# LSH attention with a routed expert layer: the second expert's number and first weight loads move ahead of the first expert's late rows

## The chip, the cores and the metric

The kernel runs on one core of a Trainium2 chip. The metric is the device time of one execution in microseconds (us). Before the change it is 733.53 us, the median of 3 runs (731.56 to 736.64). The profiled execution is a further one and took 737.76 us.

## The reference

Two stages follow one another. The first is attention over 4 batches, 8 heads, 768 positions and 64 values per head, in which a query sees only the keys of its own hash bucket (the signs of 6 projections). The second sends each of the 3072 tokens to one of 8 experts.

```python
# attention, per head
mask = q_bucket[:, :, :, None] == k_bucket[:, :, None, :]
scores = np.where(mask, scale * q @ k.T, -1e9)
x = softmax(scores) @ v                      # 3072 tokens x 512

# experts: one per token, by the largest logit
logits = x @ w_gate                          # 512 x 8
expert = argmax(logits, axis=1)
gate = softmax(logits)[token, expert]
for e in range(8):                           # w1: 512 x 1024, w2: 1024 x 512
    y[rows of e] = relu(x[rows of e] @ w1[e]) @ w2[e]
out = gate * y
```

All arrays are float32.

## The kernel before, in words

Attention works through 16 pairs of heads. Its work is issued by hand-written lists of steps (`HEAD`, `NEXT`, `PLAN`, `LAST`). Tokens are routed while attention still runs: each token's 512 values, its gate weight and its number are scattered into a DRAM table `sorted_rows` that has a region per expert (`scatter`, L501, indirect DMAs issued by POOL).

The experts are then handled one after the other, the fullest first, in phases (`PH`). Phase 0 takes the first 256 rows of the first expert, and overlaps the end of attention. Phase 1 takes its other 256 rows, the late rows. Phases 2 to 8 take one further expert each, 456 rows and fewer. Which expert comes when is known only on the chip: `rank_all` sorts the experts by their counts on DVE and writes the order to a tile `oi`, and `nc.values_load` (L562) has SP read a number out of `oi` into a register, so that later DMAs on SP can address that expert's weights.

A phase has two products. `mm1` (L774) makes eight blocks of hidden values, f = 0 to 7, each in one of three PSUM buffers named `s`. For each f, `relu` then takes the block out of PSUM twice: ACT writes the rounded value (`hh`, L788), and DVE the rest that rounding lost (L790). `mm2` multiplies by w2. In phases 0 and 1 it does so by tokens (`yout`, L831): 24 matmuls per 128 tokens, the last three of which read block f = 7. The three `s` buffers go round, so that the first `yout` of phase 1 writes the buffer that block f = 5 had.

Weights come in chunks of 128x4x512 float32: for the expert of rank r, chunks 4r and 4r+1 hold w1, chunks 4r+2 and 4r+3 hold w2. A chunk arrives in two loads of 128x2x512 (512 KB) each, which SP issues (`raw_load(c, a)`, L666) into small buffers `raw` and `raw2`. Each load has two parts, and `chunk_part(c, a)` splits a part into two tiles that TensorE multiplies: ACT rounds it (L679), POOL subtracts (L680). `halves(n, k)` splits part k of the two chunks from n on, and after each second part issues the load that takes the freed buffer. The loads of the second expert's w1 are (4, 0), (4, 1), (5, 0) and (5, 1). Parts 4 and 5 of its eight come with load (5, 0), parts 6 and 7 with load (5, 1).

`rows(n)` loads the tokens of phase n from `sorted_rows`: for phase 1 two DMAs of 128x578 float32 (L704, tile `xd`), for a later phase four of 32x16x128 (L698, tile `xg`, 256 KB each, in runs of 512 bytes) and one of 128x4x2 (L700, `xi`, in runs of 8 bytes). `xt` then transposes the late rows on TensorE (L736) in the middle of phase 0's second `yout`.

SP issues all these DMAs in program order through one queue, and an instruction that waits holds back all that stand behind it. When attention is done, its buffers are given up and a second pool (`p2`) takes their place. Tiles `raw2`, `xg`, `xi` and the later phases' tiles are in `p2`. Load (5, 0) goes to `raw2`, whose place is that of `xd`: it waits until the late rows have landed and TensorE has read them.

Of the kernel before, what the change touches and what calls it, by code (L numbers as in the profile page):

```python
# [23 lines left out]
E = 8  # L24
# [23 lines left out]
def tiles_of(n):  # L48

    return [(o, min(128, n - o)) for o in range(0, n, 128)]  # L50
# [3 lines left out]
def lsh_attention_moe(ctx, tc, qk2, v, proj, wg, w1, w1q, w2, out):  # L54
    nc = tc.nc
# [80 lines left out]
    C = {}  # L136
# [376 lines left out]
    SP = [mybir.EngineType.SP]  # L513
    EV = {}

    def keys(name):
        k = const.tile([128, E], F32, name=name)
        nc.vector.tensor_tensor(k, C["base"], C["base0"], op=OP.subtract)
        C["cnt"] = const.tile([128, E], F32, name=name + "_c")
        nc.vector.tensor_copy(C["cnt"], k)  # L520
        nc.vector.scalar_tensor_tensor(k, k, float(E), C["desc"], op0=OP.mult, op1=OP.add)
        return k
# [18 lines left out]
    def rank_all():  # L541
        k = keys("key1")
        nc.vector.scalar_tensor_tensor(k, C["first"], float(1 << 20), k, op0=OP.mult, op1=OP.add)
        g = const.tile([128, E, E], F32, name="rg")
        nc.vector.tensor_tensor(g, k[:, None, :].to_broadcast([128, E, E]), k[:, :, None].to_broadcast([128, E, E]),
                                op=OP.is_gt)
        rk = const.tile([128, E], F32, name="rk")
        nc.vector.tensor_reduce(rk, g, axis=AX.X, op=OP.add)
        ri = C["desc"]

        nc.vector.tensor_scalar(rk, rk, -1.0, float(E), op0=OP.mult, op1=OP.add)
        nc.vector.tensor_tensor(g, rk[:, None, :].to_broadcast([128, E, E]), ri[:, :, None].to_broadcast([128, E, E]),
                                op=OP.is_equal)
        C["rank_eq"] = g
        h = const.tile([128, E, E], F32, name="rh")
        nc.vector.tensor_tensor(h, g, C["desc"][:, None, :].to_broadcast([128, E, E]), op=OP.mult)
        od = const.tile([128, E], F32, name="od")
        nc.vector.tensor_reduce(od, h, axis=AX.X, op=OP.add)
        oi = const.tile([128, E], I32, name="oi")
        nc.vector.tensor_scalar(oi, od, -1.0, float(E), op0=OP.mult, op1=OP.add)  # L560
        for r in range(1, E):
            EV[r] = nc.values_load(oi[0:1, r:r + 1], engines=SP, min_val=0, max_val=E - 1)  # L562

    def spill_plan():

# [85 lines left out]
    def raw_load(c, a):  # L651

        r, k = divmod(c, 4)
        if k < 2:
            w = w1q if r else w1
            src = w[bass.ds(EV[r], 1)].rearrange("o (a p) f -> p (o a) f", p=128)[:, 2 * a:2 * a + 2,
                                                                               k * 512:(k + 1) * 512]
        else:
            o = (k - 2) * 4 + 2 * a
            src = w2[bass.ds(EV[r], 1)].rearrange("o (a p) d -> p (o a) d", p=128)[:, o:o + 2, :]  # L660
        n = 2 * c + a
        if n < 10 or n % 2:
            t = moe.tile([128, 2, 512], F32, name="raw", bufs=2)
        else:
            t = P2["p"].tile([128, 2, 512], F32, name="raw2", bufs=2)
        nc.sync.dma_start(t, src)  # L666
        RAW[c, a] = t

    def chunk_part(c, a):

        if a == 0:
            s = c % 6
            CH[c] = (moe if s < 4 else P2["p"]).tile([128, 2, 4, 512], F32R, name=CN[s])
        w, r = CH[c], RAW[c, a // 2][:, a % 2]
        if c < 4:
            nc.gpsimd.tensor_copy(w[:, 0, a], r)
            nc.gpsimd.tensor_tensor(w[:, 1, a], r, w[:, 0, a], op=OP.subtract)
        else:
            nc.scalar.activation(w[:, 0, a], r, AF.Copy)  # L679
            nc.gpsimd.tensor_tensor(w[:, 1, a], r, w[:, 0, a], op=OP.subtract)  # L680
# [8 lines left out]
    def rows(n):  # L689

        r, o, c = PH[n]
        if n > 1:
            XG[n] = P2["p"].tile([128, 16, 2 * D], F32, name="xg", bufs=2)
            XI[n] = P2["p"].tile([128, 4, 2], F32, name="xi", bufs=2)
            t = len(tiles_of(c))
            x = xsv[bass.ds(EV[r], 1), 0:128 * t]
            for a in range(4):
                nc.sync.dma_start(XG[n][32 * a:32 * a + 32, :4 * t][:, None],  # L698
                                  x[:, :, a * PW + E:a * PW + E + 2 * D].rearrange("o (g i) w -> i o g w", i=32))
            nc.sync.dma_start(XI[n][:, :t][:, None], x[:, :, GC:RW].rearrange("o (j p) w -> p o j w", p=128))  # L700
            return
        XG[n] = wk.tile([128, 2, RW], F32, name="xd")
        for j, (i, _) in enumerate(tiles_of(c)):
            nc.sync.dma_start(XG[n][:, j], xsv[bass.ds(EV[r], 1), o + i:o + i + 128].rearrange("o p w -> p (o w)"))  # L704

    def tokens(n):
        r, o, c = PH[n]
        IX[n] = moe.tile([128, 4], I32, name="ix", bufs=3)
        t = len(tiles_of(c))
        x = XI[n][:, :t, 1] if n > 1 else XG[n][:, :t, GC + 1]  # L710
        nc.vector.tensor_copy(IX[n][:, :t], x.bitcast(I32))
# [5 lines left out]
    def blocks(n, j):  # L717

        if j == 0:
            XT[n] = P2["p"].tile([128, 4, 512], F32, name="xt")  # L720
        if j < len(tiles_of(PH[n][2])):
            nc.vector.transpose(XT[n][:, :, 128 * j:128 * j + 128].rearrange("p c (t i) -> p t c i", i=32),
                                XG[n][:, 4 * j:4 * j + 4].rearrange("p t w -> p (t w)"))

    def xt(n, d):
        r, o, c = PH[n]
        if d == 0:
            XH[n] = (moe.tile([128, 2, 4, EARLY], F32R, name="xhe") if n < 2 else
                     P2["p"].tile([128, 2, 4, CAPS[1]], F32R, name="xh"))
        t = len(tiles_of(c))  # L730
        if n > 1:
            p = XT[n][:, d]
        else:
            p = ps.tile([128, 512], F32, name="t", bufs=2)
            for j in range(t):
                nc.tensor.transpose(p[:, j * 128:(j + 1) * 128], heads(XG[n][:, j], d), ident)  # L736
        if d == 0:
            GT[n] = moe.tile([128, 4], F32, name="gate", bufs=3)
            nc.vector.tensor_copy(GT[n][:, :t], XI[n][:, :t, 0] if n > 1 else XG[n][:, :t, GC])
            tokens(n)  # L740
        nc.scalar.activation(XH[n][:, 0, d, :c], p[:, :c], AF.Copy)
        nc.vector.tensor_tensor(XH[n][:, 1, d, :c], p[:, :c], XH[n][:, 0, d, :c], op=OP.subtract)  # L742
# [49 lines left out]
    def by_token(n):  # L792
        return PH[n][2] <= 384
# [288 lines left out]
    for g in range(NG):  # L1082
        for w in {0: HEAD, 1: NEXT, NG - 1: LAST}.get(g, PLAN):
# [6 lines left out]
            if g == NG - 1 and w == "R9":  # L1090
                GT[0] = moe.tile([128, 4], F32, name="gate", bufs=3)
                nc.vector.tensor_copy(GT[0][:, :2], XG[0][:, :, GC])
                tokens(0)
    rows(1)
    rank_all()
    raw_load(4, 0)
    raw_load(4, 1)
    def xts(n, ds):
        for d in ds:
            xt(n, d)  # L1100

    mm2(0, 0)
    mm2(0, 1, lambda: xts(1, (0, 1)))
    xts(1, (2, 3))
    attn.close()
    p2 = ExitStack()
# [5 lines left out]
    def halves(n, k):  # L1112

        if n < 4 * E:
            chunk_part(n + k // 4, k % 4)
            if k % 2:
                h = 2 * n + k // 2 + 3
                if h < LASTH:
                    raw_load(h // 2, h % 2)
# [6 lines left out]
    for n in range(1, len(PH)):  # L1126
        c0 = 4 * (PH[n][0] + 1)
        last = n + 1 == len(PH)
        if not last:
            rows(n + 1)  # L1130
        for f in range(8):
            mm1(n, f)
            if f % 2 and not by_token(n - 1):
                yout(n - 1, f // 2)
            halves(c0, f)
            if 3 <= n < 6:
                for _ in range(2):
                    next(plan, None)
        for m in range(4):
            mid, end = ((), ()) if last else (WHEN if n > 1 else SOON)[m]  # L1140
            if m == 0 and not last:
                for j in range(4):
                    blocks(n + 1, j)
            if not (last and m == 3):
                mm2(n, m, lambda: xts(n + 1, mid))
            halves(c0 + 2, 2 * m)
            halves(c0 + 2, 2 * m + 1)
            xts(n + 1, end)
        if n == 6:
            for _ in plan:  # L1150
                pass
        if n == 7:
            C["n"] = nc.values_load(C["cntn"][0:1, 0:1], min_val=0, max_val=TMAX)
# [65 lines left out]
```

## Time and profile before

| what | us |
|---|---|
| median of 3 runs | 733.53 |
| profiled execution | 737.76 |
| its span, first to last instruction | 735.9 |
| TensorE (PE) busy in the span | 706.5 |
| DVE busy | 490.0 |
| POOL busy | 486.3 |
| ACT busy | 413.7 |
| mean granted TensorE clock | 0.988 |

The span is what the profile's clock runs over: a moment of 461.90 is 461.90 us after the first instruction. The profiled execution takes 1.9 us more than its span, and 4.2 us more than the median of the runs. PE is the matmul side of TensorE, PEld its weight loads. SPq is SP's instruction stream; its rows are times of issue, not of transfer.

### The profile page before, as it was taken

Reading aid. Unit: us, or ns where it says so; the run is one execution under the profiler, and the core shown is the slowest. Engines: PE = TensorE matmul, PEld = TensorE weight load, DVE = VectorE, ACT = ScalarE, POOL = GpSimd, SP = SyncE. Lnnn points to the kernel's source line nnn. Section 1 sums busy time; section 2 is a strip of 40 time slices with the busy share of each in tenths; the row PEclk is TensorE's granted clock in tenths of the full one; section 3 lists DMA queues with packets and bytes.
Section 4 is the critical chain, followed back from the end, with each engine's and each line's share of the span. In section 5 each row is a group of like instructions: output and inputs, shape, how many; then the busy total and the mean of one; then the engine's idle time right before and its main releaser. Section 6 shows DMA issues by size and latency. Waiting matters only on the chain.

```text
span 735.9 us, 13469 instructions
## 1 busy us (share of the span) xinstructions
PE 706.5 (96%) x4575; PEld 571.2 (78%) x4575; DVE 490.0 (67%) x942; ACT 413.7 (56%) x836; POOL 486.3 (66%) x723
## 2 busy tenths in 40 slices
PE   8998999999999999999998999999999999999996
PEld 4766677667766776686666778799999999989895
DVE  7768898889888988998998663323666725232321
ACT  5876676677667866786676623443444444444310
POOL 8726766687778677876785664585666676768522
PEclk7999999999999999999999999999999999999998
DMA  5883788869777767797678337682737395747201
GB/s 196 289 287 78 240 242 233 250 193 257 193 214 214 221 168 224 217 257 178 193 204 219 108 133 205 193 244 88 199 132 176 135 140 180 194 145 209 75 10 39
DMA packets 69927, 135.58 MB, mean 184 GB/s; under 512 B 15571, under 2 KB 32211, under 8 KB 69856
## 3 DMA queue, kind: packets, MB, share of 16 engines
q1 hardware_dynamic: 63024, 118.31, 57.5%
q0 software_dynamic: 6688, 16.35, 6.5%
q8 instruction: 37, 0.61, 0.4%
q14 instruction: 34, 0.28, 0.1%
q10 hardware_dynamic: 144, 0.03, 0.0%
HBM read 75.79 MB, written 26.33 MB: 139 GB/s over the span
## 4 chain that ended last, share of the span: by engine, by line
PE 74%; DVE 8%; ACT 7%; issue 6%; DMA 2%; POOL 2%; SPq 1%; ACTq 0%; POOLq 0%; another core or an unknown queue 0%; DVEq 0%
PE t L407 17%; PE s L774 17%; PE s L811 10%; PE s L831 7%; PE t L346 7%; PE s L306 7%; PE s L308 6%; DVE m L316 4%; ACT e L332 4%; PE t L426 2%; DMA raw<-in_w1q_dram 1%; SPq L396 1%; ACT pt L372 1%; PE s L840 1%; ACT bits L241 1%
## 5 line engine op out<-in xcount | busy, mean ns | idle before, releaser
L332 ACT ACTIVATE e<-s,m 128x768 f32<-128x768 f32 x192 | 189.8, 992 | 80.6 <-DVE m L323 43.6
L316 DVE TENSOR_REDUCE m<-s 128x1 f32<-128x768 f32 x192 | 178.4, 947 | 14.8 <-PE s L308 9.4
L680 POOL TENSOR_TENSOR w<-raw,w 128x512 fp32r<-128x512 f32 x112 | 145.1, 1321 | 41.8 <-ACT w L679 41.0
L407 PE MATMUL t<-pt,vt 128*64 128x384 f32 x768 | 130.9, 490 | 0.2 <-DMA pt<-w 0.2
L774 PE MATMUL s<-xh,w 128*128 128x456 f32 (+6 forms) x672 | 127.0, 346 | 0.2 <-DVE xh L742 0.2
L774 PEld LDWEIGHTS s<-xh,w 128*128 128x128 f32 x672 | 119.1, 188 | 3.5 <-DVE xh L742 0.5
L790 DVE SCALAR_TENSOR_TENSOR hh<-s,hh 128x256 fp32r<-128x256 f32 (+7 forms) x64 | 35.5, 555 | 105.5 <-ACT hh L788 98.0
L346 PE MATMUL t<-ident,e 128*128 128x128 f32 x648 | 94.1, 276 | 8.3 <-ACT pt L372 2.7
L407 PEld LDWEIGHTS t<-pt,vt 128*64 128x64 f32 x768 | 52.4, 137 | 64.0 <-issue 62.7
L346 PEld LDWEIGHTS t<-ident,e 128*128 128x128 f32 x648 | 75.4, 141 | 20.7 <-ACT pt L372 6.3
L788 ACT ACTIVATE hh<-s 128x256 fp32r<-128x256 f32 (+7 forms) x64 | 31.3, 490 | 93.6 <-PE s L774 92.0
L386 DVE STREAM_TRANSPOSE w<-e 128x768 f32<-128x768 f32 x84 | 78.5, 959 | 8.2 <-ACT e L332 8.1
L811 PE MATMUL s<-hh,w 128*128 128x456 f32 (+3 forms) x384 | 74.9, 355 | 0.0
L811 PEld LDWEIGHTS s<-hh,w 128*128 128x128 f32 x384 | 71.1, 188 | 2.6
L321 POOL TENSOR_SCALAR m<-m 128x1 f32<-128x1 f32 x95 | 22.0, 232 | 75.8 <-DVE m L316 65.9
L679 ACT ACTIVATE w<-raw 128x512 fp32r<-128x512 f32 x112 | 66.4, 622 | 8.7 <-DMA raw<-in_w1q_dram 8.2
L372 ACT ACTIVATE pt<-t 128x512 f32<-128x512 f32 (+1 forms) x119 | 67.0, 586 | 6.3 <-PE t L346 5.5
L844 POOL DMA_INDIRECT out_dram<-y,ix x26 | 27.0, 1038 | 59.3 <-DVE y L842 26.0
L306 PE MATMUL s<-qk 80*128 80x384 f32 x192 | 57.1, 380 | 5.1 <-ACT e L332 4.8
L306 PE MATMUL s<-w 80*128 80x384 f32 x192 | 56.2, 374 | 5.0 <-ACT e L332 5.0
L831 PE MATMUL s<-w,hh 128*128 128x512 f32 (+1 forms) x240 | 56.7, 395 | 1.5 <-ACT hh L788 1.5
L831 PEld LDWEIGHTS s<-w,hh 128*128 128x128 f32 (+1 forms) x240 | 44.5, 187 | 12.4 <-ACT hh L788 1.9
(219 smaller groups left out, 1070.2 us busy)
## 6 DMA issues: line engine op xcount, KB each, us to landing
pt<-w SPq DMA_DIRECT2D x224, 144.0 KB
raw<-in_w_dram SPq DMA_DIRECT2D x36, 512.0 KB
raw<-in_w1q_dram SPq DMA_DIRECT2D x28, 512.0 KB
w<-in_qk_dram SPq DMA_DIRECT2D x14, 768.0 KB
xd<-in_qk_dram SPq DMA_DIRECT2D x14, 768.0 KB
sorted_rows<-xr SPq DMA_DIRECT2D x8, 1156.0 KB
vt<-in_v_dram SPq DMA_DIRECT2D x16, 384.0 KB
xg<-sorted_rows SPq DMA_DIRECT2D x16, 256.0 KB
```

The source lines that it names most:

```text
L306: nc.tensor.matmul(p[:, a, :HALF], k[0:80, 2, c], k[0:80, 3, n], start=i >= 4, stop=i < 4)
L316: nc.vector.tensor_reduce(m[:, 0:1], p[:, :, :HALF], axis=AX.XY, op=OP.max, negate=True)
L332: nc.scalar.activation(e, p[:, :, :HALF], AF.Exp, bias=m[:, 2:3], scale=m[:, 1:2], accum_out=SM[g, hf][:, t, s:s + 1])
L346: nc.tensor.transpose(p[:, x * 128:(x + 1) * 128], e[w][:, kt // 3, (kt % 3) * 128:(kt % 3) * 128 + 128], ident)
L372: nc.scalar.activation(o, x, AF.Copy)
L386: nc.vector.transpose(d.rearrange("p b k q -> p k b q"), PP.pop(i).rearrange("p a c -> p (a c)"))
L407: nc.tensor.matmul(p[s * 64:(s + 1) * 64, :HALF], VT[g][:, kt, s, :], x, start=(kt == 0), stop=(kt == NT - 1))
L679: nc.scalar.activation(w[:, 0, a], r, AF.Copy)
L680: nc.gpsimd.tensor_tensor(w[:, 1, a], r, w[:, 0, a], op=OP.subtract)
L774: nc.tensor.matmul(p[:, :c], w[:, a, d, fs], x[:, b, d, :c], start=(k == 0), stop=(k == 11))
L811: nc.tensor.matmul(p[:, :c], w[:, a, f % 4, ms], h[b][:, f, :c], start=(k == 0), stop=(k == 23))
L831: nc.tensor.matmul(p[:pw], HH[n][b][:, f, i:i + pw], w[:, a, f % 4], start=(k == 0), stop=(k == 23))
```

## The change

`rank_all` no longer loads the seven numbers. A new function `expert(r)` loads one. After attention, `rank_all` and `expert(1)` now run first, then the loads (4, 0) and (4, 1), and only then `rows(1)`. The numbers of ranks 2 to 7 are loaded in phase 1, behind `rows(2)`. In phase 1 alone, `halves` runs two parts ahead: parts 0 and 1 are split before `mm1`'s first block, part f + 2 behind block f, and nothing behind blocks 6 and 7.

```diff
-        for r in range(1, E):
-            EV[r] = nc.values_load(oi[0:1, r:r + 1], engines=SP, min_val=0, max_val=E - 1)
+        C["oi"] = oi
+
+    def expert(r):
+
+        EV[r] = nc.values_load(C["oi"][0:1, r:r + 1], engines=SP, min_val=0, max_val=E - 1)
...
-    rows(1)
     rank_all()
+    expert(1)
     raw_load(4, 0)
     raw_load(4, 1)
+    rows(1)
...
         if not last:
             rows(n + 1)
+        ahead = 2 if n == 1 else 0
+        if n == 1:
+            for r in range(2, E):
+                expert(r)
+        for k in range(ahead):
+            halves(c0, k)
         for f in range(8):
             mm1(n, f)
             if f % 2 and not by_token(n - 1):
                 yout(n - 1, f // 2)
-            halves(c0, f)
+            if f + ahead < 8:
+                halves(c0, f + ahead)
```

Only SP's and ACT's streams change; the order of instructions on PE, DVE and POOL is the same. SP's stream before, from the end of attention (`xd` is the late rows, `oi` the order of the experts, `raw`, `raw`, `raw_5697` and the last `raw` are loads (4, 0), (4, 1), (5, 0) and (5, 1); six more pairs of number loads and three more `xg` are left out):

```order
L704 DMA xd<-sorted_rows 128x578
L704 ISA
L704 DMA xd<-sorted_rows 128x578
L562 TENSOR_LOAD oi
L562 ISA x2
...
L666 DMA raw<-in_w1q_dram 128x2x512
L666 ISA
L666 DMA raw<-in_w1q_dram 128x2x512
L666 ISA
L666 DMA raw_5697<-in_w1q_dram 128x2x512
...
L700 DMA xi<-sorted_rows 128x4x2
L666 ISA
L666 DMA raw<-in_w1q_dram 128x2x512
```

SP's stream in the changed kernel (lines are 3 higher; (5, 0) is `raw_5637`; the first number load is that of rank 1, five of the six later pairs are left out):

```order
L565 TENSOR_LOAD oi
L565 ISA x2
L669 ISA
L669 DMA raw<-in_w1q_dram 128x2x512
...
L707 DMA xd<-sorted_rows 128x578
...
L669 DMA raw_5637<-in_w1q_dram 128x2x512
...
L703 DMA xi<-sorted_rows 128x4x2
L565 TENSOR_LOAD oi
L565 ISA x2
...
L669 DMA raw<-in_w1q_dram 128x2x512
```

Two weight loads now stand ahead of the late rows, and six number loads between `xi` and load (5, 1), the last of the four.

ACT's stream in phase 1 before, from the fifth block on (`hh` is a block's rounded value; `w<-raw_5697` is the split of load (5, 0), the last `w<-raw` that of load (5, 1)):

```order
L788 ACTIVATE hh_5706<-s 128x256
L679 ACTIVATE w_5796<-raw_5697 128x512
L788 ACTIVATE hh_5706<-s 128x256
L679 ACTIVATE w_5796<-raw_5697 128x512
L788 ACTIVATE hh_5706<-s 128x256
L679 ACTIVATE w_5796<-raw 128x512
L788 ACTIVATE hh_5706<-s 128x256
```

ACT's stream in the changed kernel, the same blocks (here from the third block):

```order
L791 ACTIVATE hh_5713<-s 128x256
L682 ACTIVATE w_5766<-raw_5637 128x512
L791 ACTIVATE hh_5713<-s 128x256
L682 ACTIVATE w_5766<-raw_5637 128x512
L791 ACTIVATE hh_5713<-s 128x256
L682 ACTIVATE w_5766<-raw 128x512
L791 ACTIVATE hh_5713<-s 128x256
L682 ACTIVATE w_5766<-raw 128x512
L791 ACTIVATE hh_5713<-s 128x256 x2
```

The first split of load (5, 1) stood between the blocks 6 and 7. It now stands between the blocks 4 and 5.

## Rows read from the trace of the kernel before

**Rows 1.** The page: busy us, share of the span and instructions of each engine.
```profile
PE 706.5 (96%) x4575; PEld 571.2 (78%) x4575; DVE 490.0 (67%) x942; ACT 413.7 (56%) x836; POOL 486.3 (66%) x723
```

**Rows 2.** Windows by stage: length, busy time (instructions) of each engine, clock, DMA.
```profile
440.00:476.50 36.50, 34.90 (x200) 29.73 (x198) 13.19 (x33) 14.89 (x32) 17.54 (x19) 1.00 0.69 199
476.50:720.00 243.50, 243.45 (x1291) 229.24 (x1292) 107.04 (x181) 96.95 (x192) 157.27 (x152) 1.00 0.54 147
```

**Rows 3.** Timeline of PE, 437 to 477: start, length, group, and idle time before it.
```profile
448.38 0.60 PE L736 MATMUL t<-ident,xd 128*128 128x128 f32 x4
...
450.28 11.78 PE L774 MATMUL s<-xhe,w 128*128 128x256 f32 x96
461.90 5.03 PE L831 MATMUL s<-w,hh 128*128 128x512 f32 x21
468.42 6.53 PE L831 MATMUL s<-w,hh 128*128 128x512 f32 x27 [1.50 <-ACT hh L788]
...
476.55 0.68 PE L774 MATMUL s<-xh,w 128*128 128x456 f32 x2 [0.15 <-DVE xh L742]
```

**Rows 4.** Chain of waits, 410 to 530: start, length, what the end waited for.
```profile
458.24 9.21 DMA raw<-in_w1q_dram
...
467.47 0.63 ACT w L679
468.10 0.28 ACT hh L788
```

**Rows 5.** Timeline of SP's queue, 395 to 486: start and length of issue.
```profile
443.42 0.90 SPq L704 DMA_DIRECT2D xd<-sorted_rows  x2
449.22 1.87 SPq L666 DMA_DIRECT2D raw<-in_w1q_dram  x3
451.31 4.36 SPq L698 DMA_DIRECT2D xg<-sorted_rows  x4
455.85 2.13 SPq L700 DMA_DIRECT2D xi<-sorted_rows  x1
458.24 2.36 SPq L666 DMA_DIRECT2D raw<-in_w1q_dram  x1
...
483.02 1.93 SPq L698 DMA_DIRECT2D xg<-sorted_rows  x4
485.14 0.82 SPq L700 DMA_DIRECT2D xi<-sorted_rows  x1
```

**Rows 6.** Waits of SP's queue, 405 to 500: total, times, longest.
```profile
SPq L704 <- DMA sorted_rows<-xr,slot: 18.1, 2, 16.7
```

**Rows 7.** The line of the number loads: duration (min/median/max in ns), first and last start.
```profile
L562 SPq TENSOR_LOAD <-oi x7: 261/269/481, 444.4 to 448.4; - x7
```

**Rows 8.** Timeline of DVE, 405 to 490.
```profile
440.87 0.17 DVE L560 TENSOR_SCALAR oi<-od 128x8 int32<-128x8 f32 x1
...
447.18 0.17 DVE L739 COPY gate<-xd 128x2 f32<-128x2 f32 x1 [2.51 <-DMA xd<-sorted_rows]
...
468.40 0.42 DVE L790 SCALAR_TENSOR_TENSOR hh<-s,hh 128x256 fp32r<-128x256 f32 x1 [6.91 <-ACT hh L788]
```

**Rows 9.** Windows by transfer: the last three columns are clock, DMA share, GB/s.
```profile
443.00:444.40 1.40, 1.40 (x7) 1.13 (x6) 0.48 (x1) 0.00 (x0) 0.00 (x0) 1.00 0.06 8
444.40:446.60 2.20, 2.20 (x11) 1.77 (x10) 0.27 (x1) 0.00 (x0) 1.06 (x2) 1.00 0.86 281
450.40:453.00 2.60, 2.60 (x24) 2.60 (x23) 1.43 (x4) 1.32 (x4) 0.98 (x1) 1.00 0.94 343
...
458.00:463.00 5.00, 5.00 (x39) 4.83 (x39) 1.27 (x3) 1.97 (x5) 3.19 (x3) 1.00 1.18 174
464.00:468.00 4.00, 2.92 (x13) 2.05 (x11) 0.00 (x0) 0.53 (x1) 0.00 (x0) 1.00 1.03 366
```

**Rows 10.** Windows around an earlier idle stretch of PE.
```profile
67.40:69.10 1.70, 0.04 (x7) 0.00 (x0) 1.63 (x5) 1.10 (x3) 0.88 (x2) 1.00 1.00 217
...
69.60:73.00 3.40, 3.40 (x15) 3.39 (x15) 2.21 (x6) 3.38 (x7) 2.06 (x4) 0.50 1.02 210
```

## The prediction, made before the changed kernel ran

> **What bounds the kernel now.** I read the busy table first: the matmuls fill 96% of the span, the next engine 67% [rows 1]. So only what shortens or moves TensorE's idle time can count. The table by stage then shows where that idle time is around the change: in 440 to 476.5 the matmuls are busy for 34.90 of 36.50 us, and in the 243.5 us after it for 243.45 [rows 2]. What the change could free is therefore the 1.6 us of its own stage; later stages have nothing to give, and a delay made here is not won back there.
>
> TensorE's timeline names the 1.6 us: 1.50 us before 468.42, where `yout` of the late rows waits for an ACT result, and 0.15 us before 476.55 [rows 3]. The chain of waits shows what is behind the 1.50: load (5, 1) is issued at 458.24 and lands 9.21 us later; ACT splits it (467.47) and only then takes out the last hidden block [rows 4]. SP's timeline shows why the load is late: SP does nothing from 444.32 to 449.22 but read seven numbers, and then four weight loads and all rows of the second expert go out in a heap [rows 5, 7].
>
> **SP's stream.** `oi` is written at 441.04 [rows 8]. SP is idle there: until 443.42 it waits for the scatters, the longest of the two waits being 16.7 us [rows 6]. Seven numbers take from 444.4 to 448.4 for six steps, 0.67 us each, and 0.8 us pass from the last one to the first load [rows 5, 7]. In the changed kernel one number is read at 441.1, load (4, 0) goes out at 441.9 (before: 449.22), (4, 1) at about 442.6, and the late rows at 443.42 as before. For SP this costs nothing: the wait for the scatters covers it. If the scatters landed 0.5 us earlier, the rows would be held back by the difference.
>
> **The late rows.** They now stand behind 1 MB of weights in the queue. Before, they are issued at 443.42, move from 444.4 to 446.6 at 281 GB/s [rows 5, 9], and DVE sees them at 447.18 [rows 8]; TensorE uses them at 448.38 [rows 3], 1.2 us later. In the changed kernel the weights start 1.0 us after their issue, at 442.9, and 1.05 MB at 343 to 366 GB/s [rows 9] take 2.9 to 3.1 us, until about 445.9. The 0.59 MB of rows follow at 281 GB/s: 2.1 us, and 0.6 us until they are seen, 448.6. A 256 KB output write goes on beside them and may take 0.7 us of that. TensorE then waits for 0.2 to 0.9 us. Bounds: nothing (the rows pass the weights), and 1.2 us (a slower start). I take **0.6 us**. It moves everything behind it, so below all times are relative to TensorE's.
>
> **Load (5, 0)** lies where the late rows lie, and waits for the transposes in both kernels: 450.7 (the third issue of 449.22 + 1.87 [rows 5]). It is not earlier, and `xg` and `xi` behind it are not either.
>
> **Load (5, 1)**, the one that TensorE waits for, is not issued earlier. Its buffer would be free two parts sooner, but six number loads now stand ahead of it on SP: `xg` from 451.3 for 1.93 us and `xi` 0.82 us (as in the next phase, where the queue is emptier [rows 5]), then 6 x 0.67 us, 458.3. Before: 458.24. What is gained is a shorter queue. By the rates of rows 9: the load (5, 0) moves from 451.8 on, 0.52 MB in 1.5 us; `xg`, 1.05 MB in short runs, at 174 GB/s in 6.0 us; (5, 1) in 1.4 us; 0.6 us to be seen: **461.3**. The same sum for the kernel before (1.57 MB from 450.4 in 4.5 us, then 6.0, 1.4, 0.6) gives 462.9, and it landed at 467.45 [rows 4], 4.55 us later than the sum. No row explains this lag; it could be that some DMA engines fall behind. So the lag is bounded by 0 and 4.55. It arose with 3.1 MB in the queue, and 2.1 MB are left: 4.55 x 2.1 / 3.1 = 3.1, hence landing at **464.4**; bounds 461.3 and 465.9.
>
> What a page says of such a load speaks for an earlier landing. The Trainium skill, "DMA: Bandwidth & Descriptors", section "Anatomy of one DMA", fits a DMA of its software path by about 2.0 us and the bytes at 436 GB/s, an estimated 3.2 us for 512 KB; landing would be at 461.5. This trace does not agree: the same load took 9.21 us.
>
> **ACT, two parts ahead.** The splits of (4, 0) and (4, 1) go into ACT's idle time and cost nothing. But the split of (5, 1) now stands ahead of block 5 and no longer ahead of block 7, and ACT is in order. The first `yout` needs block 5's PSUM buffer at its first matmul, 461.90; before, it needed block 7 only at its 22nd, 461.90 + 5.03 = 466.93 [rows 3]. So the deadline of the load's landing moves forward by 5 us, while the landing moves forward by about 3. From landing to the free buffer: ACT 0.63 and 0.3 us [rows 4], DVE 0.42 [rows 8], with gaps 1.5 us. TensorE waits until 464.4 + 1.5 = 465.9, that is **4.0 us** (0.9 to 5.5 by the bounds). The 1.50 us of before are gone, since the blocks 6 and 7 are ready before their matmuls come. What comes next is unchanged: the second expert's rows and weights are needed from 474.79 on and shift with TensorE, and the 0.15 us remain.
>
> **The sum.** +0.6 + 4.0 - 1.5 = **+3.1 us** (bounds: 0 + 0.9 - 1.5 = -0.6, and 1.2 + 5.5 - 1.5 = +5.2). On the profiled execution that is 737.76 + 3.1 = 740.9. This execution was 4.2 us above the median, so the forecast is 733.53 + 3.1 = **736.6 us**.
>
> **Rivals.**
> - No lag: the shorter queue has no stragglers, (5, 1) lands between 461 and 462.5, and the new wait equals the old one. -0.6 to +1.5 us, 733 to 735. For it: 174 GB/s is a mean that contains the stragglers. Against it: the 4.55 us are measured.
> - The load lands by 460.4, as the change would have it: no wait at all, -1.5 us, 732.0. It needs 0.9 us less than the sum without any lag, and no wait for the late rows.
> - My forecast, with a slower clock behind it. Where TensorE was all but idle for 1.70 us (67.4 to 69.1), its granted clock then stood at 0.50, which is 1.2 of 2.4 GHz, from 69.6 to 73.0 [rows 10]: half of 3.4 us, 1.7 us lost. The 1.50 us before 468.42 had no such effect (1.00 [rows 2]). A wait of 4 us may: +4.8, 738.3. The Trainium skill, "TensorE: Matmul & The Clock Gate", section "What's actually happening", says that the slow clock is the default and activity releases it; rows 10 agree.
> - The other side, slower by over 1%: the landing does not move at all, because the stragglers and not the megabyte set it. Then the wait is 467.45 + 1.5 - 461.9 = 7.1 us; with 0.6 to 1.2 us for the late rows, less 1.5, plus 1.7 of slow clock: +7.9 to +8.5, 741.7. It decides when (5, 1) lands later than 467 and the clock falls.
>
> **Numbers.** Forecast (+1.5 to +4.5) 0.40; no lag 0.25; slower clock 0.17; no wait 0.11; over 1% slower 0.07. The range leaves out about the last case and a part of the gain, whose runs can lie up to 2 us below: 731.5 to 740.0. The runs of before spread from 731.56 to 736.64, so that 1% (7.3 us) is what can be told from no change: below 726.2, above 740.9. A gain over 1% would need five times the idle time that is there: 0.02. Slower 0.07, the same 0.91.
>
> **What would show it.** In the changed profile: TensorE idle for some tenths before the transposes at 448.4; load (5, 1) issued near 458 to 459 behind the numbers; a wait of 1 to 5.5 us before the first `yout` of the late rows, put down to block 5 on ACT or DVE, and none in front of its 22nd matmul; 243.5 us without idle time after that. I am wrong if (5, 1) lands before 461, if `xg` moves much faster than 174 GB/s, or if idle time appears after 476.

## The result, and the profile after

The changed kernel is slower: 740.57 us (median of 6 runs, 739.05 to 743.99) against 734.36 us (6 runs), a ratio of 1.0092 with a 95% interval of 1.0071 to 1.0112. The medians are 6.2 us apart; the ratio on 734.36 us is +6.8 us (+5.2 to +8.2). A second comparison later gave 738.66 us and a ratio of 1.0059 (1.0034 to 1.0084), which is +4.3 us (+2.5 to +6.2). I had forecast 736.6 us (+3.1), with a range up to 740.0; the first measurement is 0.6 us above its end, the second lies inside. One of the ten runs of a later kernel (e2) took 1395.17 us and is left out of all figures.

The profiled execution took 740.17 us, its span 738.4 us. Its page first: the matmuls are busy 1.4 us less than before [rows 1] in a span that is 2.5 us longer, so TensorE has 3.9 us more of idle time.

```profile
PE 705.1 (95%) x4575; PEld 570.0 (77%) x4575; DVE 488.9 (66%) x942; ACT 413.7 (56%) x836; POOL 486.3 (66%) x723
```

The windows by stage, of the same two stages as [rows 2] (length, busy time and instructions of PE, PEld, DVE, ACT, POOL, then clock, DMA share, GB/s):

```profile
440.00:477.40 37.40, 32.32 (x188) 27.66 (x187) 10.80 (x25) 14.56 (x32) 15.97 (x16) 1.00 0.64 186
477.40:722.00 244.60, 244.60 (x1297) 230.07 (x1296) 108.42 (x183) 97.23 (x192) 157.33 (x152) 1.00 0.55 146
```

The added idle time is where it was expected: 5.1 us in the stage of the change (1.6 before), none in the 244.6 us behind it. PE's timeline of that stage answers to [rows 3]:

```profile
436.60 10.53 PE L834 MATMUL s<-w,qk 128*128 128x512 f32 x44
448.60 0.30 PE L739 MATMUL t<-ident,xd 128*128 128x128 f32 x1 [1.47 <-DMA xd<-sorted_rows]
449.87 0.55 PE L739 MATMUL t<-ident,xd 128*128 128x128 f32 x3 [0.96 <-DMA xd<-sorted_rows]
450.17 1.18 PE L834 MATMUL s<-w,qk 128*128 128x512 f32 x4
...
451.71 11.79 PE L777 MATMUL s<-xhe,w 128*128 128x256 f32 x96
466.16 11.36 PE L834 MATMUL s<-w,hh 128*128 128x512 f32 x48 [2.65 <-issue]
477.35 2.86 PE L777 MATMUL s<-xh,w 128*128 128x456 f32 x12
```

There are two waits. The first is for the late rows, twice, once for each of their two DMAs: 1.47 + 0.96 us. The second stands before the first `yout`, 2.65 us; the 48 matmuls behind it now run in one piece, without the 1.50 us ahead of the 22nd. "issue" means that the profile found no releaser. The rows of ACT and DVE show what PE waited for (the number in brackets is the engine's own idle time):

```profile
459.22 0.39 ACT L791 ACTIVATE hh<-s 128x256 fp32r<-128x256 f32 x1 [0.54 <-PE s L777]
464.70 0.63 ACT L682 ACTIVATE w<-raw 128x512 fp32r<-128x512 f32 x1 [5.09 <-DMA raw<-in_w1q_dram]
465.23 0.37 ACT L791 ACTIVATE hh<-s 128x256 fp32r<-128x256 f32 x1
```
```profile
465.63 0.42 DVE L793 SCALAR_TENSOR_TENSOR hh<-s,hh 128x256 fp32r<-128x256 f32 x1 [5.57 <-ACT hh L791]
```

ACT takes out block 4 (459.22), then stands 5.09 us before the split of load (5, 1). Block 5 follows at 465.23, DVE's half of it ends at 466.05 (465.63 + 0.42), and PE goes on at 466.16: it waited for block 5's PSUM buffer. The chain of waits ends in the same two places:

```profile
442.88 6.94 DMA xd<-sorted_rows
449.82 0.04 issue
449.87 0.55 PE t L739 x3
...
463.50 2.65 issue
```

SP's timeline answers to [rows 5]:

```profile
440.83 1.07 SPq L669 DMA_DIRECT2D raw<-in_w1q_dram  x2
442.31 0.91 SPq L707 DMA_DIRECT2D xd<-sorted_rows  x2
452.16 0.39 SPq L669 DMA_DIRECT2D raw<-in_w1q_dram  x1
452.76 2.25 SPq L701 DMA_DIRECT2D xg<-sorted_rows  x4
455.20 0.97 SPq L703 DMA_DIRECT2D xi<-sorted_rows  x1
459.82 0.40 SPq L669 DMA_DIRECT2D raw<-in_w1q_dram  x1
```

The stream is as read from the order. Two loads go out 8.4 us earlier than before. The late rows are issued 5.7 us after the first `yout` matmul of phase 0 (442.31 - 436.60), before 5.4 us (443.42 - 438.01). Load (5, 1) comes behind six numbers.

### The profile page after: what moved, and what is told of

Same layout as the page of the kernel before. It is cut to its first block, busy times and chain, and to the rows that moved or that the text cites. A ratio compares the mean times of both kernels' runs of the same rounds, so it can differ in the third digit from the quotient of the medians.

```text
span 738.4 us, 13472 instructions
## 1 busy us (share of the span) xinstructions
PE 705.1 (95%) x4575; PEld 570.0 (77%) x4575; DVE 488.9 (66%) x942; ACT 413.7 (56%) x836; POOL 486.3 (66%) x723
## 4 chain that ended last, share of the span: by engine, by line
PE 74%; DVE 7%; ACT 7%; issue 6%; DMA 2%; POOL 2%; SPq 2%; ACTq 0%; POOLq 0%; another core or an unknown queue 0%; DVEq 0%
PE s L777 18%; PE t L407 17%; PE s L814 10%; PE s L306 7%; PE t L346 6%; PE s L834 6%; PE s L308 6%; DVE m L316 5%; ACT e L332 4%; PE t L426 2%; SPq L396 1%; ACT pt L372 1%; PE s L843 1%; DMA xd<-sorted_rows 1%; ACT bits L274 1%
```

## The experiments

To compare traces whose attention part differs, I use one length: from the first of phase 0's 44 `yout` matmuls to phase 2's first `mm1` matmul (438.01 to 474.79 in the first trace of before, that is 36.78 us; 436.60 to 477.35 after). Beside it stands the ratio of times to the kernel before, measured on the same chip. Edits are shown against the changed kernel.

| kernel | stage, us | ratio (95% interval) |
|---|---|---|
| before, four traces | 36.78, 35.03, 35.01, 35.08 | 0.9996 (0.9975 to 1.0017), e1 |
| changed, two traces | 40.75, 39.94 | 1.0092, and 1.0059 (1.0034 to 1.0084), e8 |
| e2: late rows first | 39.52 | 1.0056 (1.0034 to 1.0077) |
| e3: splits not ahead | 36.96 | 0.9999 (0.9977 to 1.0021) |
| e4: rows, loads, numbers; splits not ahead | 35.02 | 0.9994 (0.9972 to 1.0017) |
| e5: e2 with the numbers in SP's idle time | 39.63 | 1.0064 (1.0043 to 1.0085) |
| e6: e5 with load (5, 1) ahead of xg | 34.99 | 0.9992 (0.9967 to 1.0017) |
| e7: e2 with splits one part ahead | 35.01 | 0.9988 (0.9969 to 1.0007) |
| e11: one load ahead of the rows, one part ahead | 35.35 | one run |
| e12: all of what helped | 35.02 | 0.9989 (0.9968 to 1.0009) |

The ratios tell apart a loss of 4 us, but not one of 1 us, because the runs of one kernel spread with their mean granted clock: the kernel before took 731.4 to 731.9 us at 0.999 and 735.4 to 738.0 us at 0.986 to 0.989. For small differences I therefore also give an estimate at equal clock: the distance of each run from a line through 77 runs of before (about 0.4 us per 0.001 of clock), with 95% bounds from resampling the runs.

**The kernel before, again (e1, e9, e10).** No edit.

> The kernel before, once more, for a second trace. Theory A (the changed kernel pays two new waits, about 2.4 us before the transposes of the late rows and about 2.7 us before the first yout, and the 1.5 us wait that I subtracted is not a regular part of the kernel before): a ratio of 1.000 (+-0.002), and a trace with less than 0.5 us of idle time before block 7's matmuls. Rival B (the 1.5 us are regular, and the missing 2 to 3 us of the loss are elsewhere): the same 1.2 to 1.8 us of idle time in the same place.

> A third trace of the kernel before, for one count: does TensorE wait for block 7 (1.5 us in the first trace, 0 in the second)? Theory A: the wait comes and goes with the landing of load (5, 1), between 0 and 2 us, about 1 us on average, since the kernels without it (e4, e7) are about 1 us faster than before at equal clock. Rival: it is always there or never.

> A fourth trace of the kernel before, for the same count. Theory A: a wait for block 7 of some size between 0 and 2 us, different from trace to trace. Rival: none at all (then the first trace was an accident) or 1.5 us again.

PE's timeline of e1, and ACT's split of load (5, 1):

```profile
436.71 10.54 PE L831 MATMUL s<-w,qk 128*128 128x512 f32 x44
...
447.44 1.18 PE L831 MATMUL s<-w,qk 128*128 128x512 f32 x4
...
460.61 11.29 PE L831 MATMUL s<-w,hh 128*128 128x512 f32 x48
471.74 8.53 PE L774 MATMUL s<-xh,w 128*128 128x456 f32 x39
```
```profile
464.27 0.63 ACT L679 ACTIVATE w<-raw 128x512 fp32r<-128x512 f32 x1 [4.51 <-DMA raw<-in_w1q_dram]
```

There is no wait: the load lands 3.7 us after `yout` begins (464.27 - 460.61). In the first trace that was 5.6 us (467.47 - 461.90). e9 (first two rows) and e10 are like e1, with 3.8 and 3.9 us:

```profile
459.91 11.28 PE L831 MATMUL s<-w,hh 128*128 128x512 f32 x48
463.72 0.63 ACT L679 ACTIVATE w<-raw 128x512 fp32r<-128x512 f32 x1 [4.66 <-DMA raw<-in_w1q_dram]
```
```profile
458.75 11.34 PE L831 MATMUL s<-w,hh 128*128 128x512 f32 x48
462.61 0.63 ACT L679 ACTIVATE w<-raw 128x512 fp32r<-128x512 f32 x1 [4.72 <-DMA raw<-in_w1q_dram]
```

So the 1.50 us are there in one trace of four. The limit is about 4 us, the 5.03 us of the first 21 matmuls less the 1 us that ACT takes, and three traces stay below it by a few tenths of a us only. The mean of about 1 us that I had expected (e9) is not what the four traces show. In the timed runs there are signs of a smaller mean: at equal clock, three of the four kernels without any wait in their trace are faster than the kernel before, e4 by 0.65 us (0.3 to 1.3), e7 by 0.6 us (0.3 to 1.0), e12 by 0.45 us (0.05 to 0.9), but e6 by only 0.1 us (-0.4 to 0.5).

**Late rows first (e2).**

```diff
     rank_all()
     expert(1)
+    rows(1)
     raw_load(4, 0)
     raw_load(4, 1)
-    rows(1)
```

> The changed kernel with one thing undone: the late rows go out before the loads (4, 0) and (4, 1). Theory A: no wait before the transposes, the wait before the first yout stays at 2 to 4 us, so about +3 to +4 us against the kernel before (ratio 1.004 to 1.006). Rival C (the order of the splits on ACT makes the whole loss, and the rows' wait is only moved time): +5 to +6.5 us (1.007 to 1.009), the wait before yout grown by what the transposes gave back.

```profile
449.61 11.78 PE L777 MATMUL s<-xhe,w 128*128 128x256 f32 x96
464.09 12.93 PE L834 MATMUL s<-w,hh 128*128 128x512 f32 x48 [2.69 <-issue]
476.86 5.35 PE L777 MATMUL s<-xh,w 128*128 128x456 f32 x24
```

The first wait is gone, the second has its old size, and most of the loss is still there. The `yout` stretch takes 12.93 us and not 11.36. Windows of the stretch show why (the third column from the end is the clock):

```profile
461.40:464.10 2.70, 0.01 (x1) 0.04 (x1) 0.42 (x1) 1.47 (x4) 0.76 (x1) 1.00 0.98 331
464.50:467.90 3.40, 3.40 (x10) 2.62 (x9) 3.01 (x6) 1.49 (x4) 1.38 (x3) 0.50 0.51 162
467.90:476.00 8.10, 8.10 (x37) 6.55 (x36) 1.98 (x5) 4.78 (x10) 3.44 (x3) 1.00 0.19 72
```

Behind the idle stretch the granted clock stood at 0.50, 1.2 of 2.4 GHz, and cost 1.6 us more (12.93 - 11.36). e5 shows the same behind its 2.81 us (first row below); the changed kernel shows 1.00 behind 2.65 us in its first trace and behind 2.92 us in its second, e8 (second row):

```profile
466.20:469.60 3.40, 3.40 (x10) 2.62 (x9) 2.75 (x6) 1.49 (x4) 1.13 (x2) 0.50 0.32 113
```
```profile
465.10:468.50 3.40, 3.40 (x15) 2.78 (x16) 3.15 (x6) 1.53 (x4) 1.78 (x3) 1.00 0.39 115
```

So the rival of the slow clock is real, and comes in some executions: two of four with such a wait. The Trainium skill, "TensorE: Matmul & The Clock Gate", section "What's actually happening", calls the slow clock the default that activity releases; the three rows of e2 agree.

**Splits not ahead (e3).** The order of SP stays as changed.

```diff
-        ahead = 2 if n == 1 else 0
+        ahead = 0
```

> The changed kernel with one thing undone: the splits run behind their own block again, not two parts ahead. Theory A: the wait of about 2.4 us before the transposes stays; the split of load (5, 1) is again needed 5 us later, and the load lands before that, so no wait in yout: +2.2 to +2.8 us (ratio 1.003 to 1.004). Rival D (the late landing of load (5, 1) costs whatever the order of the splits): +5 to +6.5 us.

```profile
446.54 0.30 PE L739 MATMUL t<-ident,xd 128*128 128x128 f32 x1 [0.44 <-DMA xd<-sorted_rows]
447.94 0.55 PE L739 MATMUL t<-ident,xd 128*128 128x128 f32 x3 [1.10 <-DMA xd<-sorted_rows]
...
461.42 11.28 PE L834 MATMUL s<-w,hh 128*128 128x512 f32 x48
```
```profile
462.89 0.63 ACT L682 ACTIVATE w<-raw 128x512 fp32r<-128x512 f32 x1 [2.33 <-DMA raw<-in_w1q_dram]
```

Load (5, 1) is split 1.5 us after `yout` begins, and nobody waits for it. In e1 that is 3.7 us: against TensorE the load lands 2.2 us earlier. Rival D is out. The wait for the late rows remains in the trace, and the stage is 1.9 us longer than in e1, yet the ratio is 0.9999, at most +1.5 us; theory A expected 1.003 to 1.004 and missed. e4, the next run, has no wait at all and ran beside e3 at the same mean granted clock (0.992): its median is 1.5 us lower (733.83 against 735.32), and at equal clock the estimate is 1.3 us (0.8 to 1.7). So the wait is in the timed runs, with about that size; against the kernel before it shows less, which would fit a wait in some runs of that kernel too (e1).

**The idle time of SP alone (e4).** From the kernel before: number of rank 1, late rows, two loads, six numbers, and the splits as they were.

```diff
     rank_all()
     expert(1)
+    rows(1)
     raw_load(4, 0)
     raw_load(4, 1)
-    rows(1)
+    for r in range(2, E):
+        expert(r)
...
-        ahead = 2 if n == 1 else 0
-        if n == 1:
-            for r in range(2, E):
-                expert(r)
+        ahead = 0
```

> Only the idle time of SP is used: number of rank 1, late rows, loads (4, 0) and (4, 1), then the other six numbers while SP waits for the transposes; splits behind their own block as before. Theory A: neither of the two new waits; load (5, 1) lands several us before it is needed; 0 to -1.5 us against the kernel before (ratio 0.998 to 1.000). Rival E (the DMA queue lags by itself, whatever goes ahead): a wait of 1 to 2 us before block 7's matmuls as in the first trace, ratio 1.000 to 1.002.

```profile
458.70 11.28 PE L834 MATMUL s<-w,hh 128*128 128x512 f32 x48
```

There is no wait in the stage (35.02 us); rival E, a wait before block 7 all the same, did not come. The ratio shows no gain, since the kernel before has no wait in most traces either; at equal clock the gain is 0.65 us (e1).

**Are the numbers ahead of load (5, 1) to blame? (e5)** As e2, with the numbers where e4 has them.

> As e2 (late rows first, splits two parts ahead), but the six number loads stand in SP's idle time ahead of load (5, 0), so that load (5, 1) is issued 4 us earlier. Theory F (the landing of (5, 1) is set by what stands ahead of it in the DMA queue, above all the second expert's rows in short runs, and not by when SP issues it): the wait before the first yout stays at 2.2 to 3.0 us, +3 to +4.5 us against before. Rival G (the number loads ahead of (5, 1) made it late): a wait under 1 us, +1 us or less.

```profile
455.71 2.38 SPq L669 DMA_DIRECT2D raw<-in_w1q_dram  x1
```
```profile
450.95 11.78 PE L777 MATMUL s<-xhe,w 128*128 128x256 f32 x96
465.53 12.93 PE L834 MATMUL s<-w,hh 128*128 128x512 f32 x48 [2.81 <-issue]
```

Load (5, 1) goes out 4.8 us after `mm1` begins and no longer 8.1 us as in the changed kernel (459.82 - 451.71), and the wait is 2.81 us all the same. Rival G is out: the six numbers cost nothing, the load waits in the queue.

**Load (5, 1) ahead of the second expert's rows (e6).** As e5, and further:

```diff
-        if not last:
+        if not last and n > 1:
             rows(n + 1)
...
         for k in range(ahead):
             halves(c0, k)
+        if n == 1:
+            rows(2)
```

> As e5, but the second expert's rows (xg, xi) go out behind load (5, 1) and no longer ahead of it. Theory F: (5, 1) lands 5 us or more earlier, no wait before the first yout and none before the transposes, with the splits still two parts ahead: -1.5 to 0 us against before. Rival H (splitting two parts ahead costs by itself, by ACT's time or order): +3 us or more remain.

```profile
459.69 0.63 ACT L682 ACTIVATE w<-raw 128x512 fp32r<-128x512 f32 x1 [0.95 <-DMA raw<-in_w1q_dram]
```
```profile
462.48 11.28 PE L834 MATMUL s<-w,hh 128*128 128x512 f32 x48
```

The load is split 2.8 us before `yout` begins. In the changed kernel it is split 1.4 us after the moment at which `yout` could have begun (464.70 against 463.34, which is 11.63 us behind the start of `mm1` as in e1). Two parts ahead then cost nothing: rival H is out. What stood in the load's way were the second expert's rows, the megabyte of `xg` in runs of 512 bytes and the small `xi`, which moved together.

**One part ahead (e7).** As e2, with `ahead = 1`.

> As e2, but the splits run one part ahead instead of two: the first split of load (5, 1) stands behind block 5 and ahead of block 6, whose buffer only the second yout takes. Theory (what costs is that the split stands ahead of the block whose PSUM buffer the first yout takes, so it is a step and not a slope): the wait falls from 2.7 to 0 us, -1.5 to +0.5 us against before. Rival (each part ahead costs about as much): a wait of 1.0 to 1.7 us, +1 to +2.5 us.

```profile
460.63 0.63 ACT L682 ACTIVATE w<-raw 128x512 fp32r<-128x512 f32 x1 [3.79 <-DMA raw<-in_w1q_dram]
```
```profile
459.14 11.28 PE L834 MATMUL s<-w,hh 128*128 128x512 f32 x48
```

ACT waits for the same load, 3.79 us, but behind block 5. PE waits for nothing. It is a step and not a slope: the loss hangs on which block, and so which PSUM buffer, stands behind the stalled split.

**The changed kernel again (e8).** No edit.

> The changed kernel once more, for a second trace. Theory A: both waits again, 1.5 to 2.5 us before the transposes and 2.2 to 3.2 us before the first yout; +5 to +7 us. If a stretch of slow clock follows the second wait, as in e2, the yout behind it takes 1.6 us longer. Rival: one of the two waits was an accident of the first trace and is under 0.5 us here.

```profile
447.09 0.30 PE L739 MATMUL t<-ident,xd 128*128 128x128 f32 x1 [0.23 <-DMA xd<-sorted_rows]
448.52 0.55 PE L739 MATMUL t<-ident,xd 128*128 128x128 f32 x3 [1.13 <-DMA xd<-sorted_rows]
...
465.08 11.36 PE L834 MATMUL s<-w,hh 128*128 128x512 f32 x48 [2.92 <-issue]
```

Both waits are back, 1.36 and 2.92 us. The time, +4.3 us by the ratio, is less than the +5 to +7 that I had expected.

**Half the dose (e11).** One run: only load (4, 0) stands ahead of the rows, and the splits run one part ahead.

```diff
     raw_load(4, 0)
-    raw_load(4, 1)
     rows(1)
+    raw_load(4, 1)
```

> The dose of the rows' wait: only load (4, 0), half a megabyte, stands ahead of the late rows, and the splits run one part ahead, so that the second wait is gone (e7). Theory I (the rows wait in the queue behind the weights' bytes, 1.05 MB in 4.5 us at 1.4 to 2.4 us of wait): 0.52 MB take 2.2 us less, so 0 to 0.3 us of wait before the transposes. Rival J (any load ahead of the rows costs a fixed lag of the queue): 1 us or more.

The profile names no wait, and the stage is 35.35 us, 0.3 us above that of e4. With a megabyte ahead it was 1.9 us more (e3). So in this one trace the wait follows the bytes ahead, and rival J, a fixed lag of 1 us or more, does not show.

**What the runs point to (e12).** Late rows first, numbers in the idle time, load (5, 1) ahead of `xg` (`rows(2)` behind block 0), one part ahead.

> What the runs point to: late rows first, then loads (4, 0) and (4, 1), the six numbers in SP's idle time, load (5, 1) ahead of the second expert's rows, splits one part ahead. Theory: no wait in this stage in any run, so -0.5 to -1.5 us against before (ratio 0.998 to 0.9993, at the edge of what can be told from no change). Rival (there is nothing to gain, the kernel before has no wait in most runs): 0.9995 to 1.0005.

The stage has no wait, and the ratio is 0.9989 (0.9968 to 1.0009): not told from the kernel before.

## Why the prediction was wrong

**Right: the two waits, their places and their causes, and that nothing is won back behind them.** The late rows stand behind a megabyte: with the rows first (e2, e4) that wait is gone. The deadline of load (5, 1) moves from block 7 to block 5: e3, e7 and e6 show that the second wait goes with the place of the split, by a step, or with the bytes ahead of the load. In both traces of the changed kernel the two waits make up all of the longer stage: 2.84 + 2.82 us of 5.7, and 1.77 + 3.08 us of 4.9, against the 35.04 us of the three traces of before without a wait (here a wait is counted by the starts of matmuls, which gives a few tenths more than the profile's idle time). The timed +4.3 to +6.8 us agree with that.

**The step that failed is "I take 0.6 us" for the late rows**, together with its upper bound of 1.2. From the first `yout` matmul to the first one behind the four transposes of the late rows, e1 takes 10.73 us (436.71 to 447.44) and the changed kernel 13.57 us (436.60 to 450.17): 2.84 us lost. Its second trace lost 1.77 us by the same reckoning, e3 1.95 us. The windows of the changed kernel's transfers answer to [rows 9], and DVE's row shows when the rows were there:

```profile
442.00:446.40 4.40, 4.40 (x21) 3.54 (x20) 0.75 (x1) 0.00 (x0) 1.04 (x2) 1.00 0.96 272
446.40:449.00 2.60, 1.03 (x5) 0.39 (x3) 0.00 (x0) 0.00 (x0) 0.00 (x0) 1.00 0.69 267
```
```profile
449.91 0.17 DVE L742 COPY gate<-xd 128x2 f32<-128x2 f32 x1 [6.65 <-DMA xd<-sorted_rows]
```

I priced the weights at 343 to 366 GB/s; weights, rows and the output write together moved at 267 to 272. 1.05 + 0.59 + 0.26 MB at 270 GB/s are 7.0 us, from 442 to 449.0, where the prediction has 5.0 to 5.9 us. Why the rate was lower here, and why the loss differs by 1 us between traces, is open. In the timed runs the loss is about 1.3 us (0.8 to 1.7, e3 against e4), twice the 0.6 and at the upper bound. The ratios of e8 with this wait and of e5 without it are nearly the same, but e5's trace has 1.6 us of slow clock in its place.

**"The 1.50 us of before are gone", the term "-1.5", failed too.** It took a wait of one profiled execution for a part of every execution. Three further traces have none; in the timed runs it may be half a microsecond on average (e1). I had seen that this execution stood 4.2 us above the median, and used it for the level only, not for the question whether its wait was typical. (The 4.2 us themselves go with the clock: other runs of before at the same 0.988 took 736.8 to 737.8 us.)

**"4.0 us" before `yout` was too large, for the same reason.** It is 2.65 and 2.92 us by the profile, 2.82 and 3.08 by starts. The error is in the landing: 464.4 for a `yout` at 461.90 is 2.5 us behind it, measured 1.4 and 1.6 by starts. From the landing to `yout` it is 1.5 us as predicted (464.70 to 466.16). The lag of 4.55 us that I scaled to 3.1 came from the one trace of before that had it at its largest. In e1 the load is split 15.3 us after the start of `mm1`, and my sum gives 12.6: a lag of 2.7. Scaled in the same way it is 1.8 us, the landing 463.1 and the wait 2.7 us, as measured. So the way of reckoning held here. With e1 in place of the first trace the sum would be 0.6 + 2.7 = +3.3 us, hardly another forecast: the unusual trace went in twice, with opposite signs, and that the two errors nearly cancel is luck. The miss that is left is that of the late rows.

**The lag, for which I had no row, can be counted in bytes.** From 450.00 to 467.47 the first trace moved 267 GB/s for 17.47 us, 4.66 MB. Everything up to load (5, 1), with the 256 KB output write that I had left out of this sum, is 3.41 MB. So about 1.2 MB of the loads issued behind it, from 460.79 on, had moved before it was complete. By the same count it is 0.6 to 0.8 MB in e1, e9 and e10, and 0.6 to 0.7 MB in the changed kernel. At 366 GB/s, 0.6 MB and the output write are 2.4 us, 1.2 MB and the write 4.1 us (an estimate): about the lags of 2.7 and 4.55 us. What held the load's last part back, no row shows. The fit of 3.2 us quoted in the prediction is for the software path; the profile lists these loads under `q1 hardware_dynamic`, so it does not price them. That the six numbers ahead of load (5, 1) matter, beyond its time of issue, is refuted by e5.

**The slow clock, given 0.17,** came in two traces of four with such a wait, 1.6 us each. In which of the timed runs it came is not shown. The mean clocks hint that it was in many: of the 31 timed runs of the changed kernel, e2 and e5 none is above 0.996, of the 77 of before 19 are.

**The rivals.** "No lag" and "the load lands by 460.4" are out. The other side, over 1% slower by a landing that does not move, is out too: it moved, by 2.0 to 2.5 us against `yout` (3.7 to 3.9 us behind it in e1, e9 and e10, 1.4 and 1.6 in the changed kernel).

## What to carry to other kernels

Work that is moved ahead in an engine's stream takes its wait along: before splitting "two ahead", ask which buffer stands behind the instruction that will stall, and whether what it waits for moved by as much. In a busy queue look at the bytes ahead of the transfer that is needed first: here an issue 3.4 us earlier gained nothing (e5 against e2, 4.8 and 8.2 us after the start of `mm1`), and with a megabyte less ahead the load came 4.3 us earlier (e6 against e5). A wait of one profiled execution is one sample; take a second trace of the kernel before, ahead of subtracting it or scaling it.

## What the runs showed of the hardware

- While mostly rows in runs of 512 bytes moved, the rate was 174 GB/s; with weights in runs of 2048 bytes it was 343 to 366 [rows 9]. By these rates a megabyte of the former delays what is behind it by about twice as much (an estimate).
- A load of 512 KB in a busy queue was complete only when 0.6 to 1.2 MB of the loads issued behind it had moved too (six traces, by the count above).
- An idle stretch of 2.7 to 2.9 us of TensorE was followed by the slower clock level in two executions (e2, e5) and not in two others.
